# A new emission order from the last lags on, the last skip terms summed in PSUM, the step sizes' chain ahead of the statistics and the input loaded first

## The chip, the cores and the metric

The kernel runs on one core of a Trainium2 chip. The metric is the time on the device of one execution, in microseconds. A core has five engines with queues of their own, and each works through its queue in order: TensorE (PE, with its weight loads PEld), VectorE (DVE), ScalarE (ACT), GpSimd (POOL) and SyncE (SP), which here only issues DMAs. Matmul results land in PSUM, all other tiles lie in SBUF.

## The reference

Two layers, each a state space convolution (S4) and a SwiGLU feed-forward net (FFN), each behind a LayerNorm and with a residual. The sequence has L = 2048 positions, D = 512 channels, N = 128 states per channel, and the FFN is F = 1376 wide. Both layers use the same weights.

```python
def ssm(u):
    dt = exp(log_dt)[:, None]; A = A_re + 1j * A_im
    P = exp((dt * A)[:, :, None] * arange(L))
    K = einsum("dn,dnl,dn->dl", C, P, dt * B).real
    return causal_convolution(u, K) + u * Dskip
def ffn(x): return (silu(x @ w_gate) * (x @ w_up)) @ w_down
x = A_u
for layer in range(2):
    x = x + ssm(layernorm(x))
    x = x + ffn(layernorm(x))
```

(The reference convolves by a padded FFT; `causal_convolution` stands for it.)

## The kernel before

**Start.** SP loads the step sizes `log_dt` (tile `ldt`), the first half of x into half of `xne`, the decay rates `rho` and `th`, a small table `am`, the second half of x, and then the other factors. DVE works out exp(log_dt) for the 512 channels on a 128x4 tile in some dozen small dependent operations (L164 to L174, tiles `e0`, `er_`, `ep`, `eki`), spreads the result on a diagonal (`dg`, L177), PE multiplies it with ones (`pd`, L178), and ACT copies it to `dt`. `row_stats`/`stats` (L211, L212) take mean and variance of x per row: BN_STATS, then BN_AGGR, for four rows of tiles. The rest of the program needs `dt` first in `rho * dt` (L984) and `th * dt`.

**Chunks.** The filter K is made for 64 channels at a time, 8 chunks. For each, ACT and DVE make powers of the exponentials; PE multiplies them to the taps (`lags`, tile `pk`); they are copied to `ks` and brought to the layout `kt`, by DMAs through DRAM (`spread`) in chunks 0 to 5, and by 16 selecting matmuls with the identity into `kp` and a copy (`spread_pe`) in chunks 6 and 7. `skip` (L521) adds Dskip to the taps of position 0, one row of `kt`; DVE does it, in chunk 7 POOL. `spectra` and `second`/`first_parts`/`later_parts` then make the filters' transforms on PE (`pw`) and DVE (`wo`, `wos`, L614). All of it is placed by hand: the emission order is the engines' order up to the last chunk's end.

**The transition.** From the last `lags` on, the order of the code is a list of calls: `take(g, n)` runs n steps of a generator, `split` converts FFN weights into two f16 halves (L682, L705), `scales` finds their scale, `conv[h]` is the convolution of block 0, half h of the channels (filter products L816, L819, inverse matmuls `pi`, L788, and the residual, L797), `first_parts`, `odd` and `rest` are the last filters' transforms, `norm` is the LayerNorm ahead of block 0's FFN (statistics L211, transposes `pt` L870, halves L873 and L875), and `block1` is the start of the next block's convolution.

**FFN stage.** Sequence blocks of 512 positions are worked through in the order `SEQ` of eight (layer, block) pairs. In each, `ffn` does two half-steps of 256 rows: 5 groups and a remainder of `pgu` matmuls (L934, L935, L937; the operands are split into f16 halves), on ACT a SiLU and a copy, on DVE the gating `sg` (L941) and the low half `hl` (L943), then `py` matmuls (L950 to L952), and on DVE the residual (L957). A half-step needs its norm transposed (`nn`, `nt`, L889, DMAs L891) and 2 PSUM buffers of the tag `big`, which `pgu` has in turn. The convolution of the next block (`ssm`) lies beside it. From L1253 on a scheduler places these instructions by priority, with its own model of times, so a different state at the handover can move instructions far behind it.

## Time and profile before

| | us |
|---|---|
| runs shown (median of 3; lowest, highest) | 1075.15 (1073.61, 1075.19) |
| profiled execution | 1072.84 |
| its span | 1071.1 |
| PE busy, share of the span | 1016.9 (95%) |
| DVE busy | 964.0 (90%) |
| ACT busy | 546.3 (51%) |
| POOL busy | 107.5 (10%) |

The profiled execution is 1.74 us longer than its span, and the times of single operations are those of this execution. A row of a timeline has the start, the duration, the engine, the line of the kernel, the operation, output and inputs, the output's size, and in brackets how long the engine stood idle before it and what ended that. Several equal instructions on one row have one duration from the first start to the last end. A matmul of f32 data shows as two records.

The stages in this execution: the start to about 40 us, the chunks to 237, the transition to about 345, where the last rows of block 1's first half are added, and the FFN stage to the end.

### The profile page before, as it was taken

How to read it: one execution, taken by the hardware profiler on the slowest of the kernel's cores; microseconds unless marked ns; L12 is line 12 of the kernel's file. 1: busy time of each engine (PE TensorE's matmuls, PEld its weight loads, DVE VectorE, ACT ScalarE, POOL GpSimd, SP SyncE). 2: the span in 40 equal slices, each digit the busy share in tenths (PEclk: the TensorE clock that was granted, in tenths of full speed). 3: DMA queues.
4: the chain of work that ended last, by engine and by line, in shares of the span. 5: the costliest groups of instructions: out<-in, count | busy, mean ns of one | idle time of the engine just before them, and what ended most of it. 6: DMA issues, size and time to landing. Idle time of an engine off the chain costs nothing.

```text
span 1071.1 us, 22000 instructions
## 1 busy us (share of the span) xinstructions
PE 1016.9 (95%) x8918; PEld 801.9 (75%) x8918; DVE 964.0 (90%) x1397; ACT 546.3 (51%) x1093; POOL 107.5 (10%) x169
## 2 busy tenths in 40 slices
PE   1979999998788999999999999999999999999998
PEld 1868888887686787777869687786868677696775
DVE  7999999999999999999999999999999999972221
ACT  6989888853367264466652126534526522153210
POOL 1112322320001011011000000200100000000000
PEclk9989999998899999999999999999999999999999
DMA  6366777878755354423054454453533344312000
GB/s 216 105 187 167 176 164 186 191 194 268 250 176 166 105 149 114 148 94 80 20 124 144 142 191 132 103 148 104 149 110 94 100 137 128 119 32 58 2 26 20
DMA packets 120199, 139.73 MB, mean 130 GB/s; under 512 B 50705, under 2 KB 75793, under 8 KB 119330
## 3 DMA queue, kind: packets, MB, share of 16 engines
q1 hardware_dynamic: 108098, 112.83, 35.1%
q0 software_dynamic: 12000, 25.50, 10.1%
q8 instruction: 70, 1.15, 0.5%
q14 instruction: 31, 0.25, 0.1%
HBM read 91.36 MB, written 30.67 MB: 114 GB/s over the span
## 4 chain that ended last, share of the span: by engine, by line
PE 58%; DVE 29%; ACT 5%; issue 3%; DMA 3%; POOL 1%; SPq 0%; DVEq 0%; ACTq 0%
PE pgu L934 10%; PE pgu L935 10%; PE pgu L937 10%; PE py L952 6%; PE py L951 6%; PE py L950 6%; DVE g L489 4%; PE pi L788 3%; DVE g L504 2%; DVE spare L501 2%; PE pf L284 2%; DVE wall L416 2%; DVE t L816 2%; PE pw L549 1%; DVE yk L819 1%
## 5 line engine op out<-in xcount | busy, mean ns | idle before, releaser
L934 PE MATMUL pgu<-mix,wall 128*128 128x256 f16 x1280 | 299.7, 273 | 1.6 <-ACT mix L873 1.1
L935 PE MATMUL pgu<-mix,wall 128*128 128x256 f16 x1280 | 299.5, 273 | 0.0
L937 PE MATMUL pgu<-mix,wall 128*128 128x256 f16 x1280 | 195.8, 273 | 0.0
L935 PEld LDWEIGHTS <-wall 128*128 128x128 f16 x1280 | 125.5, 98 | 17.9 <-issue 2.4
L934 PEld LDWEIGHTS <-wall 128*128 128x128 f16 x1280 | 125.4, 98 | 15.1
L937 PEld LDWEIGHTS <-wall 128*128 128x128 f16 x1280 | 125.2, 98 | 15.0
L950 PE MATMUL py<-wall,hh 128*128 128x512 f16 (+1 forms) x352 | 133.4, 379 | 0.0
L951 PE MATMUL py<-wall,hh 128*128 128x512 f16 (+1 forms) x352 | 133.4, 379 | 0.0
L952 PE MATMUL py<-wall,hl 128*128 128x512 f16 (+1 forms) x352 | 132.4, 379 | 0.0
L819 DVE TENSOR_TENSOR yk<-yk,t 128x1024 f32<-128x1024 f32 x96 | 116.9, 1218 | 0.4
L816 DVE TENSOR_TENSOR t<-uu,w 128x1024 f32<-128x1024 f32 x96 | 116.9, 1218 | 0.3
L940 ACT ACTIVATE sg<-pgu,sc 128x512 f32<-128x512 f32 x80 | 54.6, 682 | 98.1 <-PE pgu L937 95.1
L942 ACT ACTIVATE hh<-sg 128x512 f16<-128x512 f32 x80 | 50.2, 627 | 102.0 <-DVE sg L941 102.0
L941 DVE SCALAR_TENSOR_TENSOR sg<-pgu,sc,sg 128x512 f32<-128x512 f32 x80 | 59.6, 745 | 40.4 <-ACT sg L940 40.4
L549 PE MATMUL pw<-kt,ek 128*128 128x256 f32 (+1 forms) x384 | 94.0, 383 | 0.0
L549 PEld LDWEIGHTS pw<-kt,ek 128*128 128x128 f32 x384 | 75.4, 200 | 8.6
L952 PEld LDWEIGHTS <-hl 128*128 128x128 f16 (+1 forms) x352 | 34.3, 98 | 38.5
L943 DVE TENSOR_TENSOR hl<-sg,hh 128x512 f16<-128x512 f32 x80 | 54.9, 686 | 8.9 <-ACT hh L942 8.8
L951 PEld LDWEIGHTS <-hh 128*128 128x128 f16 (+1 forms) x352 | 34.5, 98 | 37.8
L950 PEld LDWEIGHTS <-hh 128*128 128x128 f16 (+1 forms) x352 | 34.4, 98 | 37.5
L514 PE MATMUL pk<-wall,g 128*32 128x64 f32 x2048 | 58.7, 287 | 1.9 <-issue 1.8
L514 PEld LDWEIGHTS pk<-wall,g 128*32 128x32 f32 x2048 | 55.9, 134 | 5.1 <-issue 5.0
(273 smaller groups left out, 1845.2 us busy)
## 6 DMA issues: line engine op xcount, KB each, us to landing
uu<-udr SPq DMA_DIRECT2D x96, 256.0 KB, 3.0
w<-wdr SPq DMA_DIRECT2D x96, 256.0 KB, 2.8
g<-g POOLq DMA_DIRECT2D x12, 512.0 KB, 7.2
udr<-fu POOLq DMA_DIRECT2D x22, 256.0 KB, 3.2
udr<-u SPq DMA_DIRECT2D x16, 256.0 KB, 3.3
kdr<-ks SPq DMA_DIRECT2D x6, 512.0 KB, 3.4
kt<-kdr SPq DMA_DIRECT2D x24, 128.0 KB, 3.1
out_dram<-xg SPq DMA_DIRECT2D x12, 256.0 KB, 2.3
```

The costliest lines, as they stand in the source:

```text
L514: PE.matmul(pk[32 * grp:32 * grp + 32, dd, :], lhsT=g[:, i, :, d], rhs=e[:, 0:64, d], start=i == 0 and dd % 8 == 0, stop=i == 1 and dd % 8 ...
L549: PE.matmul(pw[:, i], lhsT=e, rhs=kt[:, :, c + 4 * k0:4 * k1:4, :].rearrange("p g k d -> p k g d"), start=c == 0, stop=c == 3)
L816: V.tensor_tensor(t, uu.unsqueeze(2).to_broadcast([P, NQ, 2, 2, DC]), w.unsqueeze(3).to_broadcast([P, NQ, 2, 2, DC]), OP.mult)
L819: V.tensor_tensor(yk, yk, t, OP.add)
L934: PE.matmul(o, lhsT=wgu(wi, k, 0)[:, fs], rhs=nh[:, k], start=k == 0, stop=False)
L935: PE.matmul(o, lhsT=wgu(wi, k, 1)[:, fs], rhs=nh[:, k], start=False, stop=False)
L937: PE.matmul(o, lhsT=wgu(wi, k, 0)[:, fs], rhs=nlo[:, k], start=False, stop=k == 3)
L941: V.scalar_tensor_tensor(sg, pgu[:, 1], sc6[:, 4:5], sg, OP.mult, OP.mult)
L943: V.tensor_tensor(hl[:, f0:f0 + 2], sg, hh[:, f0:f0 + 2], OP.subtract)
L950: PE.matmul(py[r], lhsT=hh[:n, f, rc], rhs=wd(f, 0)[:n], start=f == 0, stop=False)
L951: PE.matmul(py[r], lhsT=hh[:n, f, rc], rhs=wd(f, 1)[:n], start=False, stop=False)
L952: PE.matmul(py[r], lhsT=hl[:n, f, rc], rhs=wd(f, 0)[:n], start=False, stop=f == FT - 1)
```

## The change

It has three parts. At the start, the second half of x is loaded right behind the first, the step sizes' chain is put into `step_sizes()`, which is called ahead of everything else under the manual schedule, and each BN_AGGR is written behind the BN_STATS of the next row. For chunks 6 and 7, `skip` is gone: POOL sets a tile of 128x512 to zero at the start, whose first row is then loaded with Dskip, and `spread_pe` adds it in PSUM by a further selecting matmul, 32 rows by 16 columns, in each of four groups. Behind the last `lags` the list of calls is written in another order, with most steps taken singly.

```diff
@@ -112,12 +112,12 @@
     def load_half(c):
         nc.sync.dma_start(xe[:, c:c + 2], x[0, c * P:(c + 2) * P, :].rearrange("(c p) d -> p c d", p=P))
     load_half(0)
+    load_half(2)
     rho = load(a_re, "rho", "u")
     th = load(a_im, "th", "u")
     am = sb.tile([P, NA + 2], I32, name="am")
     nc.sync.dma_start(am, c_am)
     sgn = am[:, NA:].bitcast(F32)
-    load_half(2)
     bw = tl([P, 2, D], "bw", "nn")
     br, bi = bw[:, 0], bw[:, 1]
     nc.sync.dma_start(br, b_re)
@@ -161,23 +161,27 @@
 
     e0, er_, ep = (sb.tile([P, 4], F32, name=f"e{i}") for i in range(3))
     eki = sb.tile([P, 4], I32, name="eki")
-    V.tensor_scalar(e0, ldt, -104.0, 89.0, OP.max, OP.min)
...
-    pd = pbig([P, D], "pd")
-    dg = tl([P, 4, P], "dg", "uu")
-    V.tensor_tensor(dg, ident.unsqueeze(1).to_broadcast([P, 4, P]), ep.unsqueeze(2).to_broadcast([P, 4, P]), OP.mult)
-    PE.matmul(pd, lhsT=ones, rhs=dg.rearrange("p c j -> p (c j)"), start=True, stop=True)
     dt = tl([P, D], "dt", "bt")
-    A.activation(dt, pd, AF.Copy)
+
+    def step_sizes():
+
+        V.tensor_scalar(e0, ldt, -104.0, 89.0, OP.max, OP.min)
...
+        pd = pbig([P, D], "pd")
+        dg = tl([P, 4, P], "dg", "uu")
+        V.tensor_tensor(dg, ident.unsqueeze(1).to_broadcast([P, 4, P]), ep.unsqueeze(2).to_broadcast([P, 4, P]), OP.mult)
+        PE.matmul(pd, lhsT=ones, rhs=dg.rearrange("p c j -> p (c j)"), start=True, stop=True)
+        A.activation(dt, pd, AF.Copy)
+
     w0 = tl([P, 2, D], "w0", "hf")
 
     def gen_w():
@@ -191,6 +195,7 @@
 
     tdk = tl([P, 2, D], "tdk", "t")
     dsk, th32 = tdk[0:1, 0], tdk[:, 1]
+    G.memset(tdk[:, 0], 0.0)
     nc.sync.dma_start(dsk, d_skip)
     dmax = sb.tile([1, 1], F32, name="dmax")
 
@@ -207,9 +212,11 @@
         mv = tl([P, 4, 2], "mv", tag)
         rs = tl([P, 8], "rs", tag)
         nb = rs[:, 4:]
-        for r in range(rows):
-            V.bn_stats(st[:, r], src[:, r])
-            V.bn_aggr(mv[:, r], st[:, r])
+        for r in range(rows + 1):
+            if r < rows:
+                V.bn_stats(st[:, r], src[:, r])
+            if r:
+                V.bn_aggr(mv[:, r - 1], st[:, r - 1])
         V.tensor_scalar(rs[:, :rows], mv[:, :rows, 1], EPS, 1.0 / scale ** 2, OP.add, OP.mult)
         G.tensor_tensor(rs[:, :rows], rs[:, :rows], mhalf[:, :rows], OP.pow)
         if then:
@@ -533,13 +540,16 @@
           for ga in range(4):
             eng.dma_start(kt[32 * ga:32 * ga + 32].rearrange("p g c d -> p g (c d)"), k[:, :, ga].rearrange("g b f -> b g f"))
 
-    def spread_pe(ks, kt):
+    def spread_pe(ch, ks, kt):
 
         kp = pbig([P, 4, 16, 16], "kp")
         for grp in range(4):
             for ga in range(4):
                 PE.matmul(kp[32 * ga:32 * ga + 32, grp], lhsT=ident[:, 32 * grp:32 * grp + 32], rhs=ks[:, ga],
-                          start=True, stop=True, tile_position=(0, 32 * ga))
+                          start=True, stop=ga > 0, tile_position=(0, 32 * ga))
+                if ga == 0:
+                    PE.matmul(kp[:32, grp, 0], lhsT=ident[:, :32], rhs=tdk[:, 0, ch * DC + 16 * grp:ch * DC + 16 * (grp + 1)],
+                              start=False, stop=True, tile_position=(0, 0))
         A.activation(kt, kp, AF.Copy)
 
     def products(pw, kt, k0, k1, q, order):
@@ -977,6 +987,7 @@
                     tops.append(m)
 
     with tc.manual_schedule(engines={mybir.EngineType.Activation, mybir.EngineType.DVE, mybir.EngineType.PE, mybir.EngineType.Pool}):
+        step_sizes()
         ts[0], ts[1] = gen_tiles(0), gen_tiles(1)
         ex = gen_exp(0, ts[0])
 
@@ -1085,8 +1096,9 @@
             at(t, lambda: box.update(pk=lags(ts[c], gs[c])))
             at(t + 7.1, copy)
             if c == NCH - 2:
-                at(t + 10.0, lambda: spread_pe(box["ks"], kt))
-            at(t + 13.1, lambda: skip(c, kt, V))
+                at(t + 10.0, lambda: spread_pe(c, box["ks"], kt))
+            if c < NCH - 2:
+                at(t + 13.1, lambda: skip(c, kt, V))
             at(t + 25.0, lambda: sizes(c, kt, box["ks"]))
             for q0, ats in list(enumerate(((t + 17.5, t + 25.2, n + 2.1, n + 7.5),
                                       (n + 6.9, n + 14.0, n + 17.3, n + 21.0))))[:2 if c < NCH - 2 else 1]:
@@ -1195,62 +1207,77 @@
         ivs = iv[0] + iv[1]
         norm = first_norm(tl([P, 2, D], "nn1", "hf"))
         last = second(*sec[-1])
+        ready, block1 = (nhl2[:, 0, 0], nhl2[:, 0, 1]), ssm(0, 1)
         take(conv[0], 1)
-        take(tail["sp"], 2)
-        spread_pe(ks, kts[1])
-        skip(c, kts[1], G)
-        take(conv[0], 1)
+        take(tail["sp"], 1)
         while tops:
             tops.pop(0)()
         scales()
-        split(1, 0)
+        spread_pe(c, ks, kts[1])
         first_parts(c, 0)
         take(conv[0], 1)
-        split(1, 1)
-        split(0, 0, 1)
-        first_parts(c, 2)
+        split(1, 0)
         split(1, 0)
         take(conv[0], 1)
+        take(tail["sp"], 1)
+        split(0, 1)
         first_parts(c - 1, 1)
+        first_parts(c, 2)
+        take(conv[0], 1)
         split(1, 0)
-        take(last, 2)
         take(conv[1], 1)
-        first_parts(c - 1, 3)
-        take(conv[1], 1)
+        take(last, 1)
+        take(last, 1)
         split(0, 1)
         split(0, 0, 1)
+        take(conv[1], 1)
         take(conv[0], 1)
         take(conv[1], 1)
-        split(1, 1)
+        split(1, 0)
+        split(1, 0)
         split(0, 0, 1)
-        take(conv[1], 1)
+        first_parts(c - 1, 3)
+        split(0, 1)
         split(0, 1)
         split(0, 0, 1)
-        take(odd, 2)
+        split(0, 0, 1)
+        take(odd, 1)
+        take(odd, 1)
         take(conv[1], 1)
+        take(conv[1], 1)
+        take(odd, 1)
         direct_size()
-        block1 = ssm(0, 1)
         take(norm, 1)
-        take(rest, 2)
+        take(rest, 1)
+        take(rest, 1)
         take(odd, 1)
-        take(odd, 2)
-        take(norm, 1)
+        take(conv[1], 1)
+        take(rest, 1)
+        take(odd, 1)
         take(block1, 1)
         take(rest, 1)
         split(1, 0)
+        take(norm, 1)
+        take(norm, 1)
         take(odd, 1)
-        take(norm, 1)
+        take(rest, 1)
         split(0, 1)
-        take(rest, 3)
+        take(rest, 1)
+        split(1, 0)
+        take(rest, 1)
+        split(0, 1)
         take(conv[0], 1)
-        take(conv[1], 1)
-        ready = nhl2[:, 0, 0], nhl2[:, 0, 1]
-        split(1, 1)
-        take(rest, 3)
-        split(1, 1)
-        take(rest, 4)
-        split(0, 0, 3)
+        take(rest, 1)
+        split(1, 0)
+        take(rest, 1)
+        split(0, 1)
+        split(0, 0, 1)
+        split(0, 0, 1)
+        take(rest, 1)
+        split(0, 0, 1)
+        take(rest, 1)
         sizes(c, kts[1], ks)
+        take(rest, 1)
         nn2 = tl([P, 2, D], "nn2", "nn")
         nt3 = sb.tile([P, D], F16, name="nt3")
         parts = itertools.cycle([nn2[:, 1].bitcast(F16)[:, i * D:(i + 1) * D] for i in range(2)] + [nt3])
```

The start on DVE, before: the rows are the last steps of the step sizes' chain (tile `e_121` is `ep`), the statistics of x, and `rho * dt`.

```order
L171 SCALAR_TENSOR_TENSOR e_121<-e_121,e_120 128x4 x3
L211 BN_STATS st<-xne 128x6
L171 SCALAR_TENSOR_TENSOR e_121<-e_121,e_120 128x4
L212 BN_AGGR mv<-st 128x2
L211 BN_STATS st<-xne 128x6
L171 SCALAR_TENSOR_TENSOR e_121<-e_121,e_120 128x4
L212 BN_AGGR mv<-st 128x2
L174 SCALAR_TENSOR_TENSOR e_121<-e_121,eki 128x4
L177 TENSOR_TENSOR dg<-ident,e_121 128x512
L211 BN_STATS st<-xne 128x6
L212 BN_AGGR mv<-st 128x2
L211 BN_STATS st<-xne 128x6
```

And after:

```order
L173 TENSOR_TENSOR e_121<-e_121,e_120 128x4
L175 SCALAR_TENSOR_TENSOR e_121<-e_121,e_120 128x4 x5
L176 TENSOR_SCALAR eki<-eki 128x4
L177 TENSOR_SCALAR eki<-eki 128x4
L178 SCALAR_TENSOR_TENSOR e_121<-e_121,eki 128x4
L181 TENSOR_TENSOR dg<-ident,e_121 128x512
L217 BN_STATS st<-xne 128x6 x2
L219 BN_AGGR mv<-st 128x2
L217 BN_STATS st<-xne 128x6
L219 BN_AGGR mv<-st 128x2
L217 BN_STATS st<-xne 128x6
L219 BN_AGGR mv<-st 128x2 x2
```

The chain and `dg` now stand together, with no statistics between their steps, and all four BN_STATS behind them.

The transition on PE: the last filter transforms (`pw`, two groups of four matmuls for each `wos`), the norm's transposes `pt`, and the FFN's first matmuls. Before:

```order
L549 MATMUL pw<-kt_423,ef 128x192
L549 MATMUL pw<-kt_423,ek_83 128x192 x3
L549 MATMUL pw<-kt_423,ef 128x192
L549 MATMUL pw<-kt_423,ek_83 128x192 x3
L549 MATMUL pw<-kt_423,ef 128x192
L549 MATMUL pw<-kt_423,ek_84 128x192 x3
L549 MATMUL pw<-kt_423,ef 128x192
L549 MATMUL pw<-kt_423,ek_84 128x192 x3
L870 MATMUL pt<-ident,nn_2652 128x128 x8
L934 LDWEIGHTS wall
L934 MATMUL pgu<-mix,wall 128x256
```

And after:

```order
L559 MATMUL pw<-kt_424,ef 128x192
L559 MATMUL pw<-kt_424,ek_84 128x192 x3
L559 MATMUL pw<-kt_424,ef 128x192
L559 MATMUL pw<-kt_424,ek_84 128x192 x3
L880 MATMUL pt<-ident,nn_2656 128x128 x8
L559 MATMUL pw<-kt_424,ef 128x192
L559 MATMUL pw<-kt_424,ek_84 128x192 x3
L559 MATMUL pw<-kt_424,ef 128x192
L559 MATMUL pw<-kt_424,ek_83 128x192 x3
L559 MATMUL pw<-kt_424,ef 128x192
L559 MATMUL pw<-kt_424,ek_83 128x192 x3
L944 LDWEIGHTS wall
```

The transposes stood behind the last `pw` group ahead of the FFN; now two more groups stand behind them and ahead of the first `pgu`.

The same place on DVE: the residual of block 0 (L797, after L807), the norm's statistics, and the subtraction that empties `pw` (L614, after L624). Before:

```order
L201 TENSOR_REDUCE dmax<-da 1x1
L211 BN_STATS st<-xg 128x6
L212 BN_AGGR mv<-st 128x2
L211 BN_STATS st<-xg 128x6
L212 BN_AGGR mv<-st 128x2
L213 TENSOR_SCALAR rs<-mv 128x2
L682 SCALAR_TENSOR_TENSOR wall<-st_2718,sc_92,wall 128x2x344 x2
L217 SCALAR_TENSOR_TENSOR rs<-mv,rs 128x2
L614 TENSOR_TENSOR wos<-pw,wos 128x2x3x64
L816 TENSOR_TENSOR yk<-u,w0r 128x1024
```

And after:

```order
L807 TENSOR_TENSOR xg<-xg,pi 128x2x256
L624 TENSOR_TENSOR wos<-pw,wos 128x2x3x64
L206 TENSOR_REDUCE dmax<-da 1x1
L217 BN_STATS st<-xg 128x6 x2
L219 BN_AGGR mv<-st 128x2 x2
L220 TENSOR_SCALAR rs<-mv 128x2
L692 SCALAR_TENSOR_TENSOR wall<-st_2781,sc_92,wall 128x2x344 x2
L224 SCALAR_TENSOR_TENSOR rs<-mv,rs 128x2
L807 TENSOR_TENSOR xg<-xg,pi 128x2x256
L624 TENSOR_TENSOR wos<-pw,wos 128x2x3x64
```

The first `wos` moved from behind the statistics and the weight pair (L682, after L692) to ahead of them, and a second one directly behind the norm's last scalar (L217, after L224).

The last block's norm on DVE, where the scheduler sets the order: `xg<-py` is the residual of the seventh block's last half-step, `nn`/`nt` are the norm of the eighth. Before:

```order
L943 TENSOR_TENSOR hl<-sg_3013,hh 128x512
L232 SCALAR_TENSOR_TENSOR rs<-mv,rs 128x2
L889 TENSOR_TENSOR nt_2989<-nn_2988 128x512
L941 SCALAR_TENSOR_TENSOR sg_3013<-pgu,sc_92,sg_3013 128x512
L889 TENSOR_TENSOR nn_2988<-nn_2988 128x512
L943 TENSOR_TENSOR hl<-sg_3013,hh 128x512
L941 SCALAR_TENSOR_TENSOR sg_3013<-pgu,sc_92,sg_3013 128x512
L232 SCALAR_TENSOR_TENSOR rs<-mv,rs 128x2
L943 TENSOR_TENSOR hl<-sg_3013,hh 128x512
L889 TENSOR_TENSOR nn_2988<-nn_2988,nt_2989 128x512
L889 TENSOR_TENSOR nt_2989<-nn_2988 128x512
L957 SCALAR_TENSOR_TENSOR xg<-py,sc_92,xg 128x512 x2
```

And after:

```order
L243 SCALAR_TENSOR_TENSOR yl_3999<-bb,sy,yl_3999 128x512
L243 SCALAR_TENSOR_TENSOR yl_3999<-mix,sy,yl_3999 128x512
L239 SCALAR_TENSOR_TENSOR rs<-mv,rs 128x2
L899 TENSOR_TENSOR nt_2996<-nn_2995 128x512
L243 SCALAR_TENSOR_TENSOR xf<-pi,sy,xf 128x2x256
L967 SCALAR_TENSOR_TENSOR xg<-py,sc_92,xg 128x512 x2
L899 TENSOR_TENSOR nn_2995<-nn_2995 128x512
L239 SCALAR_TENSOR_TENSOR rs<-mv,rs 128x2
L922 SCALAR_TENSOR_TENSOR sg_3020<-pgu,sc_92,sg_3020 128x192
L924 TENSOR_TENSOR sg_3020<-sg_3020 128x2x96
L899 TENSOR_TENSOR nn_2995<-nn_2995,nt_2996 128x512
L951 SCALAR_TENSOR_TENSOR sg_3020<-pgu,sc_92,sg_3020 128x512
```

The seventh block's residual stood behind the whole norm; now it stands ahead of three of its four `nn`/`nt` operations, and the gating passes that stood between them have moved ahead of the place shown.

More of the change, by code (lines that the diff above doesn't have):

```diff
@@ L163 @@
     eki = sb.tile([P, 4], I32, name="eki")
[L164 to L180 removed]
+    dt = tl([P, D], "dt", "bt")
+    def step_sizes():
+        V.tensor_scalar(e0, ldt, -104.0, 89.0, OP.max, OP.min)
+        V.tensor_scalar(eki, e0, 1.0 / math.log(2.0), None, OP.mult)
+        V.scalar_tensor_tensor(er_, eki, -0.693359375, e0, OP.mult, OP.add)
+        V.scalar_tensor_tensor(er_, eki, 2.12194440e-4, er_, OP.mult, OP.add)
+        V.tensor_scalar(ep, er_, 1.0 / 5040, 1.0 / 720, OP.mult, OP.add)
+        V.tensor_tensor(ep, ep, er_, OP.mult)
+        for cf in (1.0 / 120, 1.0 / 24, 1.0 / 6, 0.5, 1.0):
+            V.scalar_tensor_tensor(ep, ep, cf, er_, OP.add, OP.mult)
+        V.tensor_scalar(eki, eki, 127, 0, OP.add, OP.max)
+        V.tensor_scalar(eki, eki, 23, None, OP.logical_shift_left)
+        V.scalar_tensor_tensor(ep, ep, 1.0, eki.bitcast(F32), OP.add, OP.mult)
+        pd = pbig([P, D], "pd")
[3 more added lines that the diff above has]
+        A.activation(dt, pd, AF.Copy)
     w0 = tl([P, 2, D], "w0", "hf")
```

10 lines of the change are left out of this document (removed).

## The prediction

> **What bounds the kernel now.** I read the page first (the span and the engines' shares), then the busy time by stage, then TensorE's waits after 236 us, then the timeline round the longest of them, then VectorE at both ends of the program.
>
> ```profile
> span 1071.1 us, 22000 instructions
> ...
> PE 1016.9 (95%) x8918; PEld 801.9 (75%) x8918; DVE 964.0 (90%) x1397; ACT 546.3 (51%) x1093; POOL 107.5 (10%) x169
> ```
>
> The profiled execution took 1072.84 us, 1.74 around its span, and is 2.31 below the median of the runs shown (1075.15). I make the sum against this execution and take the difference off the median.
>
> ```profile
> 236.00:345.00 109.00, 91.45 (x773) 78.60 (x772) 105.39 (x162) 55.82 (x108) 10.09 (x10) 0.89 0.70 217
> 345.00:640.00 295.00, 295.00 (x2346) 227.76 (x2344) 292.99 (x442) 133.96 (x258) 23.28 (x33) 1.00 0.40 117
> 640.00:940.00 300.00, 299.47 (x2339) 226.06 (x2338) 297.51 (x429) 122.01 (x232) 19.84 (x29) 1.00 0.41 122
> 940.00:981.00 41.00, 41.00 (x316) 30.73 (x315) 21.87 (x37) 21.31 (x41) 1.60 (x3) 1.00 0.17 36
> 981.00:1071.10 90.10, 85.58 (x664) 63.95 (x662) 20.32 (x30) 14.75 (x24) 0.20 (x1) 0.99 0.07 21
> ```
>
> The columns are the stretch, then the busy time and the instructions of PE, PEld, DVE, ACT and POOL, then the granted clock. From 345 to 940 us PE is busy 594.5 of 595 us and DVE 290 to 297 out of 295 to 300: both are full, and neither can shorten the time alone. After 940 DVE has slack and PE has none. The transition from generating the filters to the first FFN block, 236 to 345, is where PE stands (109 - 91.45 = 17.6 us) and runs slowly (clock 0.89, which loses 0.11 x 109 = 12 us), while DVE is idle only 3.6 us.
>
> ```profile
> PE pw L549 <- DVE wos L614: 5.0, 2, 3.1
> PE pi L788 <- DVE mix L837: 4.4, 1, 4.4
> PE pi L788 <- DVE bb L837: 3.0, 1, 3.0
> PE pw L594 <- POOL kt L521: 1.8, 1, 1.8
> ...
> PE pw L549 <- DVE kt L521: 1.1, 1, 1.1
> ```
>
> These are the largest five, 15.3 us. The first two and the fourth stand in this timeline:
>
> ```profile
> 253.35 3.35 PE L541 MATMUL kp<-ks,ident 128*32 128x256 f32 x32 [1.20 <-ACT ks L525]
> 258.49 0.66 PE L594 MATMUL pw<-kt,ef 128*128 128x64 f32 x4 [1.79 <-POOL kt L521]
> ...
> 288.86 1.01 PE L549 MATMUL pw<-kt,ef 128*128 128x192 f32 x2 [3.09 <-DVE wos L614]
> 289.66 2.13 PE L549 MATMUL pw<-kt,ek 128*128 128x192 f32 x6
> ...
> 294.73 1.14 PE L549 MATMUL pw<-kt,ek 128*128 128x192 f32 x6
> ...
> 297.01 1.04 PE L870 MATMUL pt<-ident,nn 128*128 128x128 f32 x8
> 299.15 0.27 PE L934 MATMUL pgu<-mix,wall 128*128 128x256 f16 x1 [1.11 <-ACT mix L873]
> ...
> 308.75 0.60 PE L937 MATMUL pgu<-mix,wall 128*128 128x256 f16 x4
> ...
> 325.49 2.07 PE L788 MATMUL pi<-mix 128*128 128x256 f32 x4 [4.37 <-DVE mix L837]
> ```
>
> Six matmuls `pw` take 2.13 us at 289.66 and 1.14 at 294.73: the first ran at half clock. The FFN's `pgu` starts at 299.15, breaks off after eight matmuls and flows only from 308.75. What ends these waits are DVE results that stand late in DVE's order: `wos` (L614) behind the norm's statistics, `kt` behind the skip term.
>
> **The change, part by part.** *Start.*
>
> ```profile
> 5.20 0.69 DVE L211 BATCH_NORM_STATS2 st<-xne 128x6 f32<-128x512 f32 x1 [0.46 <-DMA xne<-in_A_u_dram]
> ...
> 7.06 0.69 DVE L177 TENSOR_TENSOR dg<-ident,e 128x512 f32<-128x512 f32 x1
> 8.85 0.69 DVE L211 BATCH_NORM_STATS2 st<-xne 128x6 f32<-128x512 f32 x1 [1.09 <-DMA xne<-in_A_u_dram]
> ...
> 10.67 0.69 DVE L984 TENSOR_TENSOR rho<-rho,dt 128x512 f32<-128x512 f32 x1
> ```
>
> ```profile
> 1.26 0.49 SPq L113 DMA_DIRECT2D xne<-in_A_u_dram  x1
> ...
> 3.25 0.43 SPq L113 DMA_DIRECT2D xne<-in_A_u_dram  x1
> ```
>
> ```profile
> xne<-in_A_u_dram SPq DMA_DIRECT2D x2, 512.0 KB, 4.7
> ...
> rho<-in_A_A_re_dram SPq DMA_DIRECT2D x1, 256.0 KB, 4.1
> ```
>
> The second half of x is issued seventh on this queue, at 3.25, and its statistics wait until 8.85. After the change it stands behind the first half, three issues earlier, near 1.8 us; with the 4.7 us to landing it is there near 6.5 to 7, and 7.4 if it lands as late after its issue (5.6 us) as now. The step sizes' chain no longer has two BN_STATS (0.69 and 0.66) and their aggregates among its steps, so `dg` begins near 5.6 to 5.8 instead of 7.06, and `dt`, which `rho` at 10.67 needs, is ready that much earlier. Four statistics and aggregates (3.3 us) behind `dg` end near 9.4, and `rho` starts there: **-1.25 us**. Bounds: 0, if `rho` or `th`, now issued 0.5 us later, or the half of x come late; -1.5 is the two statistics with their aggregates. DVE is over 97% busy from 40 to 345 us, so the shift is carried on.
>
> *Skip terms.*
>
> ```profile
> 237.03 0.20 DVE L521 TENSOR_TENSOR kt<-kt,tdk 1x64 f32<-1x64 f32 x1
> ```
>
> On the chain go this addition on DVE (0.20 us, with PE's wait of 1.1 for `kt`) and POOL's at 257.86 with PE's wait of 1.79 ahead of `pw` at 258.49. Added are 4 matmuls per spread, 8 records of this type; a record of `kp` takes 3.35/32 = 0.10 us at most, so 0.3 (they are narrower) to 0.85 us a spread, and I take 0.5, of which PE's waiting hides the first. DVE gains 0.2. The new zeroing of 128x512 on POOL has no row; the nearest is
>
> ```profile
> 965.59 0.20 POOL L910 MEMSET sg<- 128x128 f16 x1 [6.78 <-DVE hl L943]
> ```
>
> for 128x128 in f16. With eight times the bytes it is 0.2 to 1.6 us. POOL has nothing else to compute until the statistics are done, just ahead of 10.67 us, and the load of the skip row that waits for it on SP stands behind 8 other issues: I take nothing, and 1 us at most if that queue stood still.
>
> *New order.* The rows of before and after show what moves; the times here are worked out on the frame of before. (1) Without the skip's two waits and with `scales` ahead, `pw` begins near 256.7 (-1.8). (2) The `wos` subtraction that stood behind the statistics now stands ahead of them, as do the second halves of the first inverse transform: PE's 3.09 us of waiting goes, and so does most of the stretch at half clock behind it, 288.9 to 294.7, which loses 2.9.
>
> ```profile
> 302.98 1.22 DVE L875 TENSOR_TENSOR mix<-pt,mix 128x1024 f16<-128x1024 f32 x1
> ...
> 326.03 0.73 DVE L941 SCALAR_TENSOR_TENSOR sg<-pgu,sc,sg 128x512 f32<-128x512 f32 x1
> ...
> 366.92 0.74 DVE L957 SCALAR_TENSOR_TENSOR xg<-py,sc,xg 128x512 f32<-128x512 f32 x1
> ```
>
> (3) The norm's transposes `pt` come between `pw` groups near 290 instead of 297.0, and `nlo` (L875, 1.22 us) moves ahead of several filter passes, from 302.98 to about 296.8. (4) `pgu` then flows from about **296.8 instead of 308.75, 12 us earlier**. (5) From there DVE has to free `pgu`'s buffers, whose gating passes (L941) wait in DVE's queue between the second block's filter products. By the order the first comes near 308 instead of 326.03, so the wait of 4.37 us and the half clock behind it shrink too: 12 + 4.4 + 1 = some **17 us of lead** for PE at the end of the first half-step, whose `xg<-py` is at 366.92 now. Bounds of the lead: 9, if (5) gives 3 back, and 29, all of the stage's idle time (17.6) and lost clock (12).
>
> [...]
>
> *What limits that lead.* DVE's work is the same in sum. In 236 to 940 us it has 3.6 + 4.5 = 8.1 us of idle time to recover, and no more. What it owes PE last is the norm of the last block:
>
> ```profile
> 951.97 0.69 DVE L943 TENSOR_TENSOR hl<-sg,hh 128x512 f16<-128x512 f32 x1 [0.69 <-ACT hh L942]
> 953.32 0.75 DVE L236 SCALAR_TENSOR_TENSOR xf<-pi,sy,xf 128x512 f32<-128x512 f32 x1 [0.65 <-PE pi L788]
> ...
> 963.34 0.75 DVE L941 SCALAR_TENSOR_TENSOR sg<-pgu,sc,sg 128x512 f32<-128x512 f32 x1 [1.46 <-ACT sg L940]
> 964.01 0.68 DVE L889 TENSOR_TENSOR nn<-nn 128x512 f16<-128x512 f32 x1
> ...
> 981.11 1.41 DVE L957 SCALAR_TENSOR_TENSOR xg<-py,sc,xg 128x512 f32<-128x512 f32 x2 [6.60 <-PE py L952]
> ```
>
> ```profile
> 963.85 2.50 SPq L891 DMA_TRANSPOSE mix<-nn  x2
> ```
>
> From the residual `xf<-pi` at 953.32 to the end of the second pair of transposing DMAs (963.85 + 2.50) and its landing it is some 14.3 us; PE takes the result at 981.5. So DVE has **14 us of slack** there. In the new order 70 gating pairs stand ahead of that residual instead of 67: 3 x (0.75 + 0.69) = +4.3 us. The start and the skip give -1.4. Recovered idle time r is 0 to 8.1. The norm could thus come 11.1 + r us earlier than PE takes it now; with r near 3, 14 us. Moreover DVE's order now has both `xg<-py` of the block before (the wait at 981.11) ahead of the second `nn` (964.01), so PE's last `py` is followed by 1.4 + 0.7 + 2.5 = 4.6 us of nothing, and, as at 325.49, by some 3 us at half clock, -1.6. PE-bound that leaves 17 + 1.4 - 4.6 - 1.6 = 12.2 us; DVE-bound 14 - 1.6 = 12.4. The tail from 981 on is unchanged: 90.1 us, with PE busy 85.58.
>
> **Sum: -12 us.** 1072.84 - 12 = 1060.8 for an execution like the profiled one, 1063 against the median. Of the 12 only 1.4 come from the start and the skip; the rest is the transition.
>
> **Rivals.**
> (a) *The whole lead lands.* The scheduler leaves the norm of the last block early enough, or DVE recovers all 8.1 us and the gap there is short: -17 to -20, so 1055 to 1058. For it: DVE is idle half of the time behind 940. Against it: the `xg<-py` in its order is there to read. 0.15.
> (b) *DVE eats it.* DVE is full from 40 to 940; if it recovers nothing (r = 0), and stands at new waits for ACT's `sg` because the gating passes come too early, the norm comes 11.1 - 4 us earlier at most, and with the gap and the half clock -3 to -7 remain: 1068 to 1072. For it: 590.5 of 595 us. 0.17.
> (c) *No change in the end.* PE's lead is 9 or less and the gap at the last boundary and one or two shorter ones like it at the six other boundaries (PE has no such wait there now) take it: 1073 to 1077. 0.08.
> (d) *Slower.* The in-order wait: DVE's `nn` behind `xg<-py`. PE's last inverse matmuls `pi` stood 151 FFN matmuls ahead of the last block in the old order, and now stand among the last `py` of the block before; behind those of the first 256 rows come 44 matmuls, 5.7 us at the tail's mean of 85.58/664 = 0.13 us, or 10 if wide ones cost twice the mean, against a norm of 14.3 us. If the transition brings no lead, each such place costs 4.6 + 1.6 us, and the last boundary with a DVE that is 4.3 later some 8: 1078 to 1083. It decides if PE's lead at the end of the seventh block is under about 5 us. That would be so if the `pgu` that starts early only waits for buffers on DVE. 0.10.
>
> **How the numbers follow.** Forecast (-8 to -15 us: 1060 to 1067): 0.50. With (a) 0.15, (b) 0.17: faster 0.82; (c) same 0.08; (d) slower 0.10. About 0.2% (2.15 us) is what a measurement of this kernel can tell from no change. The predicted time is the likeliest case's, 1063. The range leaves out (d) and about half of (c), and the fastest edge of (a) beyond a lead of 20: 1055 to 1075.
>
> **What will show it.** In the profile after: the third BN_STATS without a wait and `rho` near 9.4 us; no wait for `kt` from the skip's line; PE's waits from 236 to 345 at 5 to 9 us instead of 17.6; `pgu` in flow from about 295; the first `xg<-py` near 346 instead of 366.9 with DVE still over 98% busy to 930; PE waiting 4 to 6 us ahead of the last block's first `pgu`, and the end about 90 us behind that. If `pgu` starts early and `xg<-py` comes no earlier than 360, step (5) is wrong; if PE is ahead by 17 us at 345 and by less than 8 at the seventh block's end, DVE is the bound sooner than I think; if `xg<-py` isn't waited for at the last boundary, (a) holds.

## The result, and the profile after

The changed kernel takes 1063.46 us (median of 6 runs, 1062.04 to 1065.67), the kernel before 1074.62 in the same comparison (6 runs). The ratio is **0.9902**, with a 95% interval from 0.9890 to 0.9913: 11.2 us, or 1.0%, faster. The forecast was 1063.

The page of the changed kernel, its span and the engines' busy time:

```profile
span 1060.2 us, 22043 instructions
...
PE 1011.7 (95%) x8934; PEld 797.7 (75%) x8934; DVE 961.6 (91%) x1396; ACT 544.9 (51%) x1093; POOL 108.9 (10%) x169
```

The span is 10.9 us shorter (1071.1 before). PE's busy time falls by 5.2 us though it has a little more to do: a matmul at half clock counts as busy for longer (six `pw` took 2.13 us at half clock and 1.14 at full clock before), so this is stretches at half clock that are gone.

Busy time by stage, with the columns of before (stretch, PE, PEld, DVE, ACT, POOL, granted clock):

```profile
236.00:345.00 109.00, 100.97 (x920) 84.13 (x920) 106.02 (x166) 57.53 (x112) 7.05 (x7) 0.98 0.69 219
345.00:640.00 295.00, 292.54 (x2311) 224.51 (x2309) 291.11 (x439) 139.99 (x275) 23.21 (x34) 1.00 0.39 118
640.00:930.00 290.00, 288.59 (x2291) 221.60 (x2289) 287.50 (x419) 112.62 (x211) 22.35 (x27) 1.00 0.40 121
```

In the transition PE's busy time rises from 91.45 to 100.97 us of 109 and its clock from 0.89 to 0.98. Behind it PE now stands a little (2.5 and 1.4 us where it stood 0.0 and 0.5), and DVE is nearly as full as before (578.6 of 585 us from 345 to 930, 580.6 before).

DVE at the start:

```profile
5.68 0.69 DVE L181 TENSOR_TENSOR dg<-ident,e 128x512 f32<-128x512 f32 x1
...
7.57 0.66 DVE L217 BATCH_NORM_STATS2 st<-xne 128x6 f32<-128x512 f32 x1
...
9.24 0.69 DVE L995 TENSOR_TENSOR rho<-rho,dt 128x512 f32<-128x512 f32 x1
```

`dg` begins at 5.68 (before: 7.06), the third BN_STATS has no wait, and `rho` stands at 9.24 instead of 10.67: 1.43 us.

PE in the transition:

```profile
250.41 0.65 PE L548 MATMUL kp<-ks,ident 128*32 128x256 f32 x8 [1.20 <-ACT ks L532]
250.87 0.21 PE L551 MATMUL kp<-tdk,ident 128*32 128x16 f32 x2
...
253.73 0.66 PE L604 MATMUL pw<-kt,ef 128*128 128x64 f32 x4 [1.16 <-ACT kt L553]
...
277.69 4.28 PE L798 MATMUL pi<-bb,mix 128*128 128x256 f32 x16 [2.80 <-DVE bb L847]
...
288.31 1.04 PE L880 MATMUL pt<-ident,nn 128*128 128x128 f32 x8
...
294.40 0.60 PE L947 MATMUL pgu<-mix,wall 128*128 128x256 f16 x4 [0.28 <-DVE mix L885]
```

The new skip matmuls are the rows `kp<-tdk`. The wait for POOL's skip is gone (253.73 waits for the copy instead), `pt` stands at 288.31 instead of 297.01, ahead of the last three `pw` groups (the rows of the order after show three behind it, not two), and `pgu` flows from 294.40 instead of 308.75. Two waits for the inverse transform's `bb` remain, one of them shown. On DVE, the first gating pass and the first residual of the first half-step:

```profile
304.73 0.74 DVE L951 SCALAR_TENSOR_TENSOR sg<-pgu,sc,sg 128x512 f32<-128x512 f32 x1
...
346.84 0.75 DVE L967 SCALAR_TENSOR_TENSOR xg<-py,sc,xg 128x512 f32<-128x512 f32 x1
```

The first gating pass was at 326.03 and the residual at 366.92. PE's lead is 366.92 - 346.84 = 20.1 us here. It doesn't reach the end whole. These are PE's waits from 345 us on (us in total, times, longest):

```profile
PE pgu L913 <- DMA mix<-nn: 2.7, 2, 1.5
PE pgu L944 <- DVE sg L922: 1.7, 2, 1.0
PE pgu L915 <- DMA mix<-nt: 1.0, 1, 1.0
PE pgu L944 <- DVE sg L951: 0.9, 1, 0.9
PE pi L798 <- DVE yl L243: 0.8, 1, 0.8
PE pgu L915 <- DMA mix<-nn: 0.5, 1, 0.5
```

The three waits of the first and the third row stand at the start of the last block. The other rows, 3.9 us in sum, stand between 400 and 692 us; from there to 965 no wait of PE is listed. DVE, SP's transposing DMAs and PE at the last boundary:

```profile
951.57 1.41 DVE L243 SCALAR_TENSOR_TENSOR yl<-bb,sy,yl 128x512 f16<-128x512 f32 x2
...
956.86 0.75 DVE L243 SCALAR_TENSOR_TENSOR xf<-pi,sy,xf 128x512 f32<-128x512 f32 x1 [3.27 <-PE pi L798]
...
964.92 1.40 DVE L967 SCALAR_TENSOR_TENSOR xg<-py,sc,xg 128x512 f32<-128x512 f32 x2
966.24 0.68 DVE L899 TENSOR_TENSOR nn<-nn 128x512 f16<-128x512 f32 x1
```

```profile
967.36 2.52 SPq L901 DMA_TRANSPOSE mix<-nn  x2
```

```profile
955.45 1.36 PE L798 MATMUL pi<-yl,mix 128*128 128x256 f16 x11
...
964.66 0.38 PE L962 MATMUL py<-wall,hl 96*128 96x512 f16 x1
966.15 0.26 PE L913 MATMUL pgu<-wall,mix 128*128 128x192 f16 x1 [1.11 <-DMA mix<-nn]
...
967.45 0.26 PE L915 MATMUL pgu<-wall,mix 128*128 128x192 f16 x1 [0.96 <-DMA mix<-nt]
...
969.99 0.34 PE L913 MATMUL pgu<-wall,mix 128*128 128x192 f16 x1 [1.54 <-DMA mix<-nn]
```

And the busy time of the same stretch, with the clock in the sixth column behind it:

```profile
968.00:970.00 2.00, 0.46 (x7) 0.23 (x4) 0.00 (x0) 1.94 (x6) 0.00 (x0) 0.95 0.77 207
970.00:972.00 2.00, 2.00 (x11) 1.49 (x12) 0.16 (x1) 0.42 (x3) 0.70 (x1) 0.50 0.29 56
972.00:974.00 2.00, 2.00 (x17) 1.89 (x16) 0.00 (x0) 0.39 (x2) 0.00 (x0) 0.70 0.00 0
```

The seventh block's last residual is at 964.92 instead of 981.11, so 16.2 us of the lead are left, 20.1 less the 3.9 of waits on the way. But the norm of the last block is late: its residual `xf<-pi` comes at 956.86 (before: 953.32), its last transposing DMA ends at 969.88, and PE waits 1.11 + 0.96 + 1.54 = 3.6 us for its pieces. Then PE runs at half clock from 969.8 to 973.2, which loses 1.7. 16.2 - 3.6 - 1.7 = 10.9 us, the difference of the spans.

What sets the start of that norm stands in the same rows. DVE stood idle for 3.27 us ahead of `xf<-pi`, waiting for PE's inverse matmuls `pi`. DVE's `yl`, which these read, were done at 952.98; eleven of the `pi` begin only at 955.45, because they stand among the `py` of the seventh block in PE's own order, without a wait of PE. Behind them PE has 8.2 us of work left in this block (956.81 to 965.04), and the norm takes 13.0 us from `xf<-pi` to its last DMA, as long as before (953.32 to 966.35). So at this place the chain runs from PE's order through the norm back to PE, and DVE's load isn't what it waits for. In all four profiles with this order of the FFN stage (the changed kernel, its repetition, order alone, order and start, see below) the three waits come to 3.6 us, though the first residual stands at 346.84, 347.37, 350.64 and 349.39.

### The profile page after: what moved, and what is told of

The parts are those of the page before. It is cut to its first block, busy times and chain, and to the rows that moved or that the text cites. A ratio compares the mean times of both kernels' runs of the same rounds, so it can differ in the third digit from the quotient of the medians.

```text
span 1060.2 us, 22043 instructions
## 1 busy us (share of the span) xinstructions
PE 1011.7 (95%) x8934; PEld 797.7 (75%) x8934; DVE 961.6 (91%) x1396; ACT 544.9 (51%) x1093; POOL 108.9 (10%) x169
## 4 chain that ended last, share of the span: by engine, by line
PE 38%; DVE 24%; ACT 4%; issue 3%; DMA 3%; POOL 0%; SPq 0%; DVEq 0%; ACTq 0%
PE pgu L944 7%; PE pgu L945 7%; PE pgu L947 7%; PE py L960 4%; PE py L962 4%; PE py L961 4%; DVE t L826 3%; DVE yk L829 3%; DVE yk L826 3%; PE pi L798 2%; DVE sg L951 2%; DVE hl L953 1%; PE pf L291 1%; DVE yl L243 1%; ACT junk L236 1%
## 5 line engine op out<-in xcount | busy, mean ns | idle before, releaser
L559 PE MATMUL pw<-kt,ek 128*128 128x256 f32 (+1 forms) x384 | 91.8, 376 | 0.0
L559 PEld LDWEIGHTS pw<-kt,ek 128*128 128x128 f32 x384 | 73.2, 195 | 9.0
```

The source lines that it names most:

```text
L559: PE.matmul(pw[:, i], lhsT=e, rhs=kt[:, :, c + 4 * k0:4 * k1:4, :].rearrange("p g k d -> p k g d"), start=c == 0, stop=c == 3)
```

## The experiments: the parts alone

**The start alone**, in the old order with the old skip:

```diff
     load_half(0)
+    load_half(2)
...
+        step_sizes()
         ts[0], ts[1] = gen_tiles(0), gen_tiles(1)
...
+        for r in range(rows + 1):
+            if r < rows:
+                V.bn_stats(st[:, r], src[:, r])
```

> The kernel before with the start of the change alone (second half of x first, unbroken chain, statistics behind it). Theory A (the start shifts everything behind it, and nothing gives it back): rho's product at 9.2 us instead of 10.7, the last lags 1.3 us earlier, time -1.3 us against before (ratio 0.9988). Rival B (PE's waits in the transition are set by something that doesn't shift with DVE, such as a DMA): rho early, but 0 at the end. Caveat for both: the scheduler orders the FFN stage anew, which can add or take some us.

Measured: 1073.33 us against 1074.83, ratio 0.9984 (0.9972 to 0.9996), or -1.5 us. Theory A holds, within an interval of -0.4 to -3.0 us; that the FFN stage was ordered anew cost or gave nothing that can be seen.

**The skip terms in PSUM alone:**

```diff
-                          start=True, stop=True, tile_position=(0, 32 * ga))
+                          start=True, stop=ga > 0, tile_position=(0, 32 * ga))
+                if ga == 0:
+                    PE.matmul(kp[:32, grp, 0], lhsT=ident[:, :32], rhs=tdk[:, 0, ch * DC + 16 * grp:ch * DC + 16 * (grp + 1)],
...
-        skip(c, kts[1], G)
```

> The kernel before with the skip terms of the last two chunks in PSUM, and the old order and start. Theory A: both waits for kt (1.1 and 1.8 us) go, the copy of kt stays, the new matmuls cost about 0.2 us a spread; PE stands as long at its next waits for DVE, so pgu flows 0 to 1 us earlier than 308.75 and the time changes by 0 to -1.5 us. Rival B (the waits for kt were on the path that sets the end): -2 to -3 us.

Measured: 1069.93, ratio 0.9953 (0.9939 to 0.9968), -4.9 us with 3.3 to 6.6 in the interval. Theory A underrates it, and so does the rival. Both waits are gone from its profile, 2.9 us in sum, but the first residual is only 0.8 us earlier (366.09 against 366.92), and other executions with the old order up to there had it at 369.1 and 371.55. The rest may be the FFN stage, which the scheduler ordered anew; this run alone can't tell.

**The order alone**, and **order and start together**. From 284 us on, the instructions of PE, DVE and ACT stand in both in the order of the changed kernel, so no new order of the FFN stage is mixed into the differences. The second one's edit of the changed kernel, in part:

```diff
-        spread_pe(c, ks, kts[1])
+        spread_pe(ks, kts[1])
+        skip(c, kts[1], G)
         first_parts(c, 0)
```

> The kernel before with the new list of calls alone: old start, and skip on DVE and POOL. The FFN stage stands in the same order as in the changed kernel. Theory A (the order makes nearly all of the gain): first xg<-py near 349 instead of 366.9, time -8.5 to -10 us against before (ratio 0.991 to 0.992). Rival B (the order needs the free kt to pay): less than -6 us.

> New start and new order, skip terms on DVE and POOL as before. Same order in the FFN stage as the changed kernel. Theory A: 1.3 us less than order alone, and 0.2 to 1 us more than the changed kernel: about -10 us (ratio 0.9905 to 0.991), since the wait for POOL's skip delays only pw, and DVE sets the pace behind it. Rival B (the skip's wait costs its 1.8 us at the end): -8.5 to -9 us.

Measured: order alone 1067.52, ratio 0.9934 (0.9916 to 0.9952), -7.3 us, between the two theories; with the start 1066.13, ratio 0.9917 (0.9902 to 0.9932). The start adds 1.4 here too. With it, -8.7 us lie in rival B's range, and the interval takes in theory A's -10 as well. The step from there to the changed kernel is the skip: 0.9917 to 0.9902, or to 0.9893 when it was measured again, so 1.6 to 2.6 us, with intervals that overlap. The profile of order and start:

```profile
251.36 3.48 PE L547 MATMUL kp<-ks,ident 128*32 128x256 f32 x32 [1.20 <-ACT ks L531]
256.38 0.66 PE L600 MATMUL pw<-kt,ef 128*128 128x64 f32 x4 [1.53 <-POOL kt L527]
```

`pw` begins at 256.38 there and at 253.73 in the changed kernel, 2.65 us apart, and 2.55 us of it are left at the first residual (349.39 to 346.84). Of the 2.65, 1.0 us comes from ahead of `kp` (PE's wait of 0.8 for DVE's skip of chunk 6 is in it), 0.4 from the wait for POOL, and the remaining 1.3 from `kp` itself, which ran at half clock in this execution. That last part isn't the skip's: in the run with a filler (below) `kp` ran at half clock with the skip in PSUM, and `pw` began at 255.63. So the skip is worth 1.4 us by the profile, more than theory A's 1 and less than rival B's 1.8, and by the medians somewhat more than either; which of the two is right stays open. What is plain is that DVE doesn't hide the whole of it.

So the parts are about **-1.4 us (start), -2 (skip, 1.4 to 2.6) and -7.3 (order, 5.2 to 9.0 in the interval)**, and add up to the whole within what can be told.

## The experiments: what limits the lead

Extra work was put into the fourth block, in the old and in the new order: 4.3 us on PE (matmuls whose result is overwritten), or some 3.6 to 4.1 us on DVE (a subtraction that is repeated):

```diff
+                for _ in range(10 if (layer, b) == (1, 0) and r + f == 0 else 0):
+                    PE.matmul(py[r], lhsT=hh[:n, f, rc], rhs=wd(f, 0)[:n], start=True, stop=True)
```

```diff
-                    V.tensor_tensor(hl[:, f0:f0 + 2], sg, hh[:, f0:f0 + 2], OP.subtract)
+                    for _ in range(4 if (layer, b) == (1, 0) and f0 == 0 else 1):
+                        V.tensor_tensor(hl[:, f0:f0 + 2], sg, hh[:, f0:f0 + 2], OP.subtract)
```

> The changed kernel with 10 more py matmuls in each half-step of the fourth block, 20 x 0.2155 = 4.3 us of PE work and nothing for DVE. Theory A (in the changed kernel the last block starts when DVE's convolution and the norm behind it are done, and PE has some 5 us to spare there): 0 to +1.5 us against the changed kernel's 1063.5, so 1063.5 to 1065 and the wait ahead of the last block's pgu smaller by about 4 us. Rival B (PE's own work sets the end, the gap at the last boundary being a fixed cost behind PE): +4.3 us, 1067.8. Caveat for both: the scheduler orders what lies behind anew.

> The changed kernel with one hl subtraction of the fourth block repeated three times in each half-step: 6 x 0.6 to 0.69 = 3.6 to 4.1 us of DVE work and nothing for PE. Theory A: +3 to +4 us against the changed kernel, 1066.5 to 1067.5. Rival B: 0 to +1 us. Caveat as before.

> The kernel before with the same 4.3 us of PE work. Both theories: PE was the bound there at the last boundary, so +4 to +4.5 us against the kernel before (ratio 1.0037 to 1.0042). A smaller rise would say that PE had slack in the old order too.

> The kernel before with the same 3.6 to 4.1 us of DVE work. Theory A (DVE had 14 us of slack at the last boundary): 0 to +1 us (ratio 1.000 to 1.001). Rival C (DVE, full from 40 to 940 us, also set the pace of the old order): +3 to +4 us.

Measured, as ratios to the kernel before: changed kernel with PE work 0.9885 (0.9863 to 0.9907), with DVE work 0.9903 (0.9880 to 0.9926); kernel before with PE work 1.0056 (1.0036 to 1.0075), with DVE work 1.0010 (0.9999 to 1.0021).

By the times, PE work costs nothing in the changed kernel (0.9885 against 0.9902) and does in the kernel before, as theory A says and rival B doesn't; DVE work is nearly free in the kernel before, against rival C. But DVE work was to cost 3 to 4 us in the changed kernel and cost 0 to 1, where rival B had 0 to 1. And the times alone mislead: the scheduler ordered all four anew, DVE's instructions in about a hundred places, beginning at 603 to 656 us. In the changed kernel with PE work, `pi` now stand far ahead of the last `py`:

```profile
957.09 1.36 PE L798 MATMUL pi<-yl,mix 128*128 128x256 f16 x11
...
972.77 0.38 PE L964 MATMUL py<-wall,hl 96*128 96x512 f16 x1
```

Some 14.7 us of PE work lie behind them instead of 8.2, the norm's last DMA ends at 970.71, and PE neither waits at the last boundary nor runs at half clock there. The seventh block's last residual is 7.6 us later than in the changed kernel (972.54 against 964.92), so the added work did arrive there; the gap and its half clock, 5.3 us, are gone; and 7.6 - 5.3 = 2.3 us is the difference of the spans (1062.5 and 1060.2). So the work wasn't hidden in spare time of PE: the new order took the gap out.

In the run with DVE work DVE's last convolution and norm are late as expected:

```profile
960.51 0.74 DVE L243 SCALAR_TENSOR_TENSOR xf<-pi,sy,xf 128x512 f32<-128x512 f32 x1
...
969.87 0.69 DVE L899 TENSOR_TENSOR nn<-nn 128x512 f16<-128x512 f32 x1 [1.87 <-DMA mix<-nn]
```

3.6 us each against 956.86 and 966.24. What that costs at the end is blurred by the new order, and by the clock, whose half-rate stretch there is 3.4 or 6.8 us long (below). So the extra work doesn't show which engine has room, and rival B isn't refuted by it for an order that stays the same. The rise of 6.9 us for PE's 4.3 in the old order isn't clean either: its profile has the first residual later already, ahead of the added work,

```profile
371.55 0.73 DVE L959 SCALAR_TENSOR_TENSOR xg<-py,sc,xg 128x512 f32<-128x512 f32 x1
```

by 4.6 us against 366.92, by waits and clock in the same transition, and its order is another from 656 us on.

**The norm taken out of the way.** The last block's first norm is computed from rows that are ready early:

```diff
-        xt = xs[HOME[SEQ.index((layer, b))]][:, s * rows:(s + 1) * rows]
+        xt = xs[HOME[SEQ.index(SEQ[-2] if (layer, b) == SEQ[-1] and s == 0 else (layer, b))]][:, s * rows:(s + 1) * rows]
```

> The changed kernel, in which the last block's norm of its first 256 rows is taken of the block before it, whose rows are ready some 40 us earlier; this leaves out that the last block's FFN is fed its own rows. Theory A (the end of DVE's last convolution and the norm behind it cost the last boundary 3.6 us of waiting and 1.7 us of clock): no wait ahead of the last block, -4.5 to -5.5 us against the changed kernel of the same call, about 1058. Rival B (PE's own work sets the end and the gap is made up for elsewhere): 0 to -1 us.

**PE kept busy in the gap.**

```diff
+                if f0 == FT - 1 and (layer, b) == SEQ[-1] and s == 0:
+                    for _ in range(16):
+                        PE.matmul(pgu[:, 0].rearrange("p a t -> p (a t)"), lhsT=hh[:, 0, :P], rhs=wd(0, 0), start=True, stop=True)
```

> The changed kernel with 16 matmuls of 128x512 (16 x 0.2155 = 3.4 us), whose result is overwritten, ahead of the last block's first pgu, where PE waits 1.1, 1.0 and 1.5 us for the norm and then runs at half clock for 3.4 us. Theory A (the waits are for the norm and the half clock is the price of the idle time): the norm's last piece still lands at the same time, the clock stays at 1.00 there, -1.2 to -1.7 us against the changed kernel of the same call. Rival B (PE's own work sets the end): +3 us. Rival C (the half clock comes anyway): 0 to +1 us.

**The changed kernel again**, unchanged, beside these.

> The changed kernel itself, as the measure for the three others of this call: ratio 0.9902 again (0.989 to 0.9913). Theory on the clock: the stretches at half clock in the transition fall differently from one execution to the next, so the first xg<-py comes within 2 us of 346.8 but not at the same time.

Measured side by side: the changed kernel again 1063.84 us, ratio 0.9893 (0.9877 to 0.9909); with the early norm 1057.25, 0.9833 (0.9818 to 0.9848); with the filler 1061.51, 0.9875 (0.9861 to 0.9890).

The early norm gives 6.6 us more, against 4.5 to 5.5 expected and 0 to 1 by the rival: theory A. DVE in that run:

```profile
935.77 0.69 DVE L899 TENSOR_TENSOR nn<-nn 128x512 f16<-128x512 f32 x1
...
964.62 0.75 DVE L967 SCALAR_TENSOR_TENSOR xg<-py,sc,xg 128x512 f32<-128x512 f32 x1 [3.22 <-PE py L962]
```

The `nn` that stood at 966.24 is at 935.77, and DVE waits for PE's `py` at the last boundary, as in the old order. PE shows no wait at all between 940 and 985. The gain fits what the gap cost in the changed kernel beside it, 3.6 us of waits and 3.4 by half clock. The order up to 922 us is that of the changed kernel, and little moves behind it, so this run is the clean one: with the norm early, the gap is gone. It doesn't tell what makes the norm late, since with the norm it takes away both DVE's residual and PE's `pi` ahead of it.

The filler gives 2.3 us more by the medians (1.2 to 1.7 expected; the intervals overlap, so the profile has to carry the reading), though it is work that is thrown away. PE in that run, and the clock in the stretch that was at 0.50:

```profile
965.59 3.62 PE L938 MATMUL pgu<-wall,hh 128*128 128x512 f16 x16
...
970.72 0.26 PE L913 MATMUL pgu<-wall,mix 128*128 128x192 f16 x1 [0.52 <-DMA mix<-nn]
```

```profile
970.00:972.00 2.00, 1.48 (x15) 1.02 (x13) 0.02 (x1) 1.11 (x3) 0.70 (x1) 1.00 0.40 77
```

The 16 matmuls end ahead of the norm's last pieces, one wait of 0.52 us is left in this view, and the clock stays at 1.00, where it fell to 0.50 in all four profiles with this order and no filler. Rivals B and C fall. In the second execution of the changed kernel the same stretch was worse than in the first:

```profile
970.00:972.00 2.00, 0.88 (x5) 0.72 (x6) 0.00 (x0) 1.50 (x5) 0.36 (x1) 0.52 0.62 120
972.00:974.00 2.00, 2.00 (x13) 1.55 (x11) 0.16 (x1) 0.00 (x0) 0.34 (x1) 0.50 0.00 0
974.00:976.00 2.00, 2.00 (x12) 1.54 (x11) 0.42 (x1) 1.04 (x3) 0.00 (x0) 0.50 0.00 0
```

Half clock lasts from 970 to past 976 here instead of 3.4 us. The span was 1062.6 us instead of 1060.2; 1.1 of that was there ahead of the gap (the last `xg<-py` of the seventh block at 966.04 instead of 964.92), the other 1.3 came behind it. The clause on the first residual held too (347.37).

**One step of the list undone:**

```diff
-        take(odd, 1)
         direct_size()
         take(norm, 1)
+        take(odd, 1)
```

> The changed kernel with one step of its list undone: the first wos subtraction stands behind the norm's statistics and the weight pair again, 4.3 us later on DVE. Theory A (step 2 of the prediction): a wait of 3 to 4 us for wos returns on PE ahead of the third pw group, pt near 292 instead of 288.3, pgu flows 2 to 4 us later and the first xg<-py comes 2 to 4 us later; of that PE's slack at the last boundary hides up to 5 us, so the time changes by 0 to +2.5 us. Rival B (the place of wos doesn't matter, since pt waits for the norm anyway): first xg<-py within 0.7 us. The scheduler orders the FFN stage anew.

Measured: 1059.99 us, ratio 0.9858 (0.9841 to 0.9875), **3.9 us faster** than the changed kernel beside it. Both theories miss. The wait for `wos` that returns is small:

```profile
285.52 0.59 PE L559 MATMUL pw<-kt,ef 128*128 128x192 f32 x2 [1.03 <-DVE wos L624]
```

1.03 us instead of 3 to 4, and `pt` comes at 289.52, as in the changed kernel's second execution (289.17). So step 2 of the prediction, taken by itself, is worth about 1 us on PE, and the first residual isn't later (345.72). The gain comes later: the scheduler ordered the FFN stage anew, and DVE stands less. The two stages in this run, and the second one in the changed kernel:

```profile
236.00:345.00 109.00, 100.03 (x912) 83.30 (x911) 106.87 (x168) 57.09 (x111) 5.36 (x7) 0.98 0.69 219
345.00:930.00 585.00, 582.91 (x4620) 448.36 (x4618) 580.59 (x859) 255.35 (x488) 44.84 (x61) 1.00 0.41 120
```

```profile
345.00:930.00 585.00, 581.14 (x4599) 446.11 (x4597) 578.62 (x857) 252.62 (x486) 45.57 (x61) 1.00 0.40 120
```

DVE is idle 2.1 + 4.4 = 6.5 us from 236 to 930, against 3.0 + 6.4 = 9.4 in the changed kernel. Its last convolution and norm come that much earlier:

```profile
954.26 0.75 DVE L243 SCALAR_TENSOR_TENSOR xf<-pi,sy,xf 128x512 f32<-128x512 f32 x1 [2.82 <-PE pi L798]
...
963.64 0.69 DVE L899 TENSOR_TENSOR nn<-nn 128x512 f16<-128x512 f32 x1
```

`xf<-pi` 2.6 us earlier than in the changed kernel's first execution and 3.7 earlier than in its second (957.98), `nn` 2.6 and 3.7. The work is the same in amount. But PE's order is another too: its waits from 345 to 960 us come to 2.0 us instead of 3.9, those at the last boundary to 1.9 instead of 3.6, and the clock stays full there. Whether DVE's smaller idle time brings this or PE's order does isn't told apart; ahead of `xf<-pi` DVE waits for `pi` here too (2.82 us). Filler and this order both beat the changed kernel; the two together were not tried.

## Why the prediction held, step by step

**The time and the outline of its mechanism were right**: PE's lead from the transition, cut at the last block's norm, -12 us foretold and -11.2 measured. What makes the norm late was read wrongly, and part of the agreement is luck. On PE the prediction had 18.4 us of lead (17 + 1.4), nothing lost on the way, and 4.6 + 1.6 at the last boundary: 12.2. The profile has 20.1, 3.9 lost on the way, and 3.6 + 1.7: 10.9. More lead and a smaller gap make up for most of the waits that weren't counted. That the sum by DVE's slack gave nearly the same, 12.4, is chance: that slack didn't set the end.

- Start: -1.25 us foretold, -1.4 and -1.5 measured. The half of x was there when DVE came to it.
- Skip terms: only the 0.2 us of DVE's addition were counted in the sum, against 1.4 to 2.6 measured; in the old order, alone and with the FFN stage ordered anew, even 3.3 to 6.6. PE's two waits were taken to be covered by DVE, and they aren't, or not wholly.
- Order: the remaining 10.6 us foretold, 7.3 measured. Its early part was right (`pgu` flowing from 296.8 foretold, 294.40 seen; the first gating pass 308 foretold, 304.73 seen) and the lead of the order alone was 16.3 us (first residual at 350.64) where 17 were foretold.
- The waits for `wos` (step 2): their disappearance was put down to one subtraction moved ahead of the statistics. Put back, it costs 1.03 us. The rest of what was booked there belongs to the order as a whole; which step of it brings most was not taken apart further.
- DVE's recovered idle time r: 3 us foretold, none found. From 236 to 930 DVE was idle 109 - 105.39 + 585 - 580.64 = 8.0 us before and 9.4 after. The last residual moved from 953.32 to 956.86, not because DVE was full there but with a wait of 3.27 us for PE's `pi` ahead of it.
- The gap at the last boundary: 4.6 us and 1.6 of clock foretold, 3.6 and 1.7 seen. Its cause was named wrongly. DVE's `xg<-py` stands ahead of `nn`, but ACT had `nn`'s input ready only at 965.85, so `nn` at 966.24 lost at most 0.4 us by it. What is late is the whole norm, which begins when PE's `pi` are done and then has only 8.2 us of PE's work beside it. The prediction had this in rival (d), which put 5.7 to 10 us of matmuls behind `pi` against a norm of 14.3, and didn't take it into its sum. Other runs bear it out: the same gap in four profiles of this order, and none where the scheduler left 14.7 us behind `pi`. A run that moves nothing but `pi` was not made.
- Rival (a), the whole lead, is what the early norm gives (1057.25, foretold 1055 to 1058): it needs the gap to be gone. The sign that was to show it, no wait for `xg<-py` at the last boundary, was there without it, since the gap has another cause. Rival (b), that DVE eats the lead, happened in part: 3.4 us of waits for DVE's `sg` and `yl` behind 345 us. Rivals (c) and (d) would have needed a lead under 9 and under 5 us.
- The clock: half clock was foretold behind the gap, and came, though the longest single gap is 1.54 us. From 965 to 970 PE was busy 1.4 of 5 us, between three gaps of 1.11, 0.96 and 1.54. The Trainium skill ("TensorE: Matmul & The Clock Gate", Part 1, HAM oscillation) warns of gaps over 3.4 us; by these rows three shorter ones within 5 us did it too.

## What to carry to other kernels

Where two engines are full side by side, a lead gained on one can be lost at the last place where it takes the other's result. Follow the chain behind that place back before you name its cause: here the fuller engine was itself waiting, and the delay began in the first engine's own order. Adding work to each engine in turn is a cheap way to tell, but only if the order stays the same; taking the suspected dependency out was the clearer way here. And a scheduler behind a hand-made order answers each change of it: isolate a part in a version whose later order stays the same, or the rest of the difference can't be assigned.

## What the runs showed of the hardware

Executions of one program differ in where PE's half-clock windows fall. The changed kernel ran at half clock for 3.4 us at the last boundary, and in another execution for over 6; `kp` of the transition ran at half clock in some executions and at full clock in others. Each is worth 1.3 us or so in one place, as much as the smallest part of this change. And sixteen matmuls without use, put where PE would stand, kept the clock at 1.00, and the program was no slower for them, by the medians 2.3 us faster.
